# One kernel of linear attention and two gated layers: first loads split, gate work moved between VectorE and GpSimd, and the planner's numbers set anew

## The chip, the cores and the metric

The kernel runs on one core of a Trainium2 chip. The metric is the device time of one execution in microseconds (us). A core has five engines that run their own queues in order: TensorE (PE in the profile, its weight loads PEld), VectorE (DVE), ScalarE (ACT), GpSimd (POOL) and SyncE (SP), which here issues every DMA. They wait for each other through semaphores.

## The reference

Three stages follow each other. All data is float32, except the weights, which arrive as float64.

```python
# attention: B=4, H=8, S=768 steps, D=48
for t in range(S):
    state = alpha[:, :, t, :, None] * state + einsum('bhd,bhe->bhde', k[:, :, t], v[:, :, t])
    y[:, :, t] = einsum('bhd,bhde->bhe', q[:, :, t], state)
x = y with its heads side by side              # 3072 tokens x 384
# first layer, d_ff = 2048
h = x @ w_in
g = (a[0] + a[1]*h + a[2]*h**2 + a[3]*h**3) / (1 + abs(b[0])*abs(h) + abs(b[1])*h**2 + 1e-6)
x = g @ w_out
# second layer, d_ff = 2048
h = x @ w_in2
out = (h * tanh(softplus(h))) @ w_out2
```

## The kernel before, in words

The 768 steps are cut into six blocks of 128, and each block holds 512 tokens (4 batches of 128). Attention of a block is two units (`attn_unit`, two batches each): twelve units in all. Inside a unit the steps stand in chunks of 64, and within a chunk the decays are handled by doubling: six levels (1, 2, 4, 8, 16, 32), at each of which TensorE makes a triangle of scores (line 444), VectorE scales queries and keys by products of decays (lines 451, 457), and VectorE or, for the levels 16 and 32, ScalarE writes the scores into the matrix AT (lines 477, 472, 466). Ahead of the levels stands the product of queries and keys themselves (line 412), and the first scaling of half of the queries by the decays (line 418). After the levels come transposes of the keys (505, copied by ScalarE at 509), the chunk's state (520), the state's decay on GpSimd (529) and its gain on VectorE (534), the outputs (555 or 591), and copies by ScalarE (612, 616) into `xf`, the input of the first layer. For the first unit ScalarE copies the first chunk's state at line 544. Queries (`QC`), keys (`K`) and decays (`al`) of a unit lie in one tile `qka` of 128 x 3 x 1024; the second unit borrows the tile `zp` for it.

A layer runs over a block in 16 steps. A step is nine matmuls of 512 columns into one PSUM bank (`hidden_mms`, line 632), the gate on the other engines, and nine matmuls into three output banks (`out_mms`, line 681). Nine, because float32 is kept by splitting input and weights into a rounded high part and the rest: three products for each of three slices. In the first layer the gate is the rational function: ScalarE takes |h| into `u` (647), B1*|h|+B0 into `z` (653), GpSimd multiplies z by u (654); or, where `E_M` has a V for the block, ScalarE makes B1*|h| from the bank (649) and VectorE adds and multiplies (650). ScalarE makes A3*h (655), VectorE two steps of the polynomial (656, 658), ScalarE log and exp of the denominator (660, 664), VectorE the last step (665). In the second layer it is one activation (669). In both, the result is split (`split_g`): the high part by a cast `gh` (helper line 215 on ScalarE, 217 on VectorE), the rest by a subtraction `gl` (helper line 208 on VectorE, 210 on GpSimd). `E_GL` says by layer and block which of the two engines subtracts.

The weights come as float64 and are converted on the chip during the first blocks: ScalarE (320, 333, 334) and VectorE (336, or 322 to 326) put the bits together, a cast makes the high part, and the low part is made on TensorE with a copy by ScalarE (344, 345, 348) or by a subtraction on VectorE (208), as `E_LW` says. Low parts go to DRAM and are streamed back for each later block.

All of this is recorded first and put in order afterwards by `Plan.order`, a list scheduler: each operation has a due time, worked out from the numbers at the head of the file (`T0`, `T_PH`, `AT_P0`, `LAG` and so on), and on each engine the ready operation with the earliest due time is taken. So the numbers set the order of every queue. The planner also puts small matmuls without use on TensorE's queue (line 725) until the first layer begins. The blocks of the two layers are run in the order of `PHASES`, (layer, block): (0,0), (0,1), (1,0), (0,2), (1,1) and so on, with the attention of the next block between the matmuls.

Of the kernel before, what the change touches and what calls it, by code (L numbers as in the profile page):

```python
# [15 lines left out]
ALU = mybir.AluOpType  # L16
# [9 lines left out]
NTOK = B * P  # L26
# [9 lines left out]
NLVM = 5  # L36
T0 = 34.498
PHASES = ((0, 0), (0, 1), (1, 0), (0, 2), (1, 1), (0, 3), (1, 2), (0, 4), (1, 3), (0, 5), (1, 4), (1, 5))
T_PH = (8.299, 4.563, 4.71, 6.475, 6.278, 6.257, 9.331, 8.784, 5.935, 5.739, 5.256, 2.662)
AT_P0 = (0.424, -13.295, 0.991)  # L40
AT_P1 = (0.528, 1.587, 0.282)
AT_P = (0.554, 1.217, 0.317)
D_MID = 8.38
LAG = (27.598, 7.732)
D_SPL = (1.238, -1.451)
W_LEAD = 13.438
X_LEAD = 139.18
D_W1 = (-0.027, 22.996)
D_W2 = (22.28, 21.655)
E_LO = 'VV'  # L50
E_TREE, E_QK = ('PPPVPV', 'VVVVVP')
E_M = 'PPVPPV'
E_GL = ('PVPVVV', 'VVVVPP')
R_PSUM = [0, 0, 0, 0, 0, 0]
NWL, NWO = 8, 8
N16 = 20
C_PED = 2
N_PRE = 8
E_LW = 'PPPPPPPPVVVVVVVVVVVVVVVVVVVVVVVV'
E_HC = 'AAAAAAAVAAVAAAAAAAAAAVVAAVVVVVVA'  # L60
E_X0 = 'A'
E_CV = 'AAAAAAAAAAAADDDDDDDDDDDDDDAADDAA'
R0 = (34.089, 17.077)
NDIAG = 20
NRAW, NF32 = 2, 2
D_X = 88.596
D_EV = 0.91
F_OPEN = 5.16
F_END = 110.537
F_RATE = 1281.623  # L70
D_CST = -48.973
NZ, NG, NU = 4, 3, 3
# [5 lines left out]
class Plan:  # L78
# [11 lines left out]
    def __init__(self):  # L90
        self.ops, self.writer, self.readers = [], {}, {}
        self.filler = None

# [17 lines left out]
    def order(self):  # L111
        ops = self.ops
# [5 lines left out]
        free, port = {}, 0.0  # L118
        ready = {}
        ops = self.ops = list(ops)  # L120
        events = [(1.9, 1, n) for n in range(len(ops)) if not left[n]]
        heapq.heapify(events)
        out, busy, loaded = [], {}, 0
        fill, lit = self.filler, 1e9
        while events:
            t = events[0][0]
            while events and events[0][0] <= t + 1e-9:
                _, kind, n = heapq.heappop(events)
                if kind == 0 and fill and n == fill[5]:
                    lit = max(fill[1], t + 2.7)  # L130
                    heapq.heappush(events, (lit, 2, -1))
                if kind == 1:
                    heapq.heappush(ready.setdefault(ops[n][0], []), (ops[n][2], n))
            if fill and lit <= t < fill[2] and free.get("PE", 0.0) <= t + 1e-9 and not ready.get("PE"):
                tick = int(t / self.TICK)
                if busy.get(tick, 0) < fill[3] * (t - tick * self.TICK + fill[0]):
                    ops.append(("PE", fill[0], 0.0, set(), fill[4], False, 1.0, None))
                    users.append([])
                    ready.setdefault("PE", []).append((0.0, len(ops) - 1))
                else:  # L140
                    heapq.heappush(events, (t + 0.1, 2, -1))
            for eng, q in ready.items():
# [3 lines left out]
                while q:  # L146
# [7 lines left out]
                    if eng == "PE":  # L154
                        if us == 0.680:
                            fill = None
# [26 lines left out]
def attention_moe_kernel(ctx: ExitStack, tc: tile.TileContext,  # L183
# [35 lines left out]
    def dma(kb, due, reads, writes, emit):  # L219
        plan.add("SP", max(0.42, kb / 300.0), due, reads, writes, emit, False, 2.5)  # L220
# [148 lines left out]
    def attn_unit(b, c, bf, due):  # L369
# [20 lines left out]
        def now():  # L390
            return due(k[0] / steps)

        dma(1573, now() - 8, [], [kQC, kK, kal], lambda: nc.sync.dma_start(out=bf.qka, in_=qka[u]))
        if c >= C_PED:
# [243 lines left out]
    def hidden(l, hb, r, i, due):  # L638
# [7 lines left out]
        if l == 0:  # L646
# [5 lines left out]
            else:  # L652
# [7 lines left out]
            act(NTOK, due, [], [kz], lambda: nc.scalar.activation(zs[r], zs[r], AF.Ln, bias=c_1), src="s", ptr=1, table="ln")  # L660
            kw = kh if R_PSUM[c] else kz
            w = lambda: h if R_PSUM[c] else zs[r]
            act(NTOK, due, [kz], [kw] + (["tab"] if last else []),
                lambda: nc.scalar.activation(w(), zs[r], AF.Exp, scale=-1.0), src="s", table="ln")  # L664
            dve(NTOK, due, [kw], [kp], lambda: nc.vector.scalar_tensor_tensor(  # L665
                out=ps[r], in0=ps[r], scalar=A0, in1=w(), op0=ALU.add, op1=ALU.mult), port=not R_PSUM[c], ptr=1)
        else:
# [195 lines left out]
```

## Time and profile before

| | us |
|---|---|
| median of 3 runs (1012.78 to 1016.35) | 1014.22 |
| the profiled execution | 1018.92 |
| its span, first to last instruction | 1017.1 |
| first matmul of the first layer begins | 80.14 |
| TensorE busy | 977.7 |
| VectorE busy | 653.1 |
| ScalarE busy | 647.4 |
| GpSimd busy | 254.4 |

The profiled execution is one run, 4.7 us above the median of the others. A busy TensorE is not one at full speed: the profile's busy time of a matmul overlaps that of the next, and holds what the clock costs. Idle time of another engine costs nothing as long as TensorE has work.

### The profile page before, as it was taken

The page shows a single profiled execution, that of the slowest core. Times are in us where ns is not written, and L with a number is a line of the kernel's source. Part 1 is how long each engine was busy: PE and PEld are TensorE (multiplying, and loading weights), DVE is VectorE, ACT ScalarE, POOL GpSimd, SP SyncE. Part 2 cuts the span into 40 slices and gives each one's busy share as a digit, 9 for nine tenths or more (in the row PEclk, how much of TensorE's full clock was granted, in tenths as well). Part 3 has the DMA queues.
Part 4 walks back from the last instruction along what each step waited for, and adds up shares of the span by engine and source line. Part 5 has one row for each costly group of instructions (what it writes and reads, how often), then busy time and mean ns, then how long its engine had stood idle before and what let it go on. Part 6 is the DMA issues. An engine that isn't in the chain of part 4 may idle for free.

```text
span 1017.1 us, 25314 instructions
## 1 busy us (share of the span) xinstructions
PE 977.7 (96%) x10744; PEld 788.2 (77%) x10744; DVE 653.1 (64%) x850; ACT 647.4 (64%) x1130; POOL 254.4 (25%) x202
## 2 busy tenths in 40 slices
PE   7999969899999999999999999999999999999998
PEld 6767757678788778888778887878778878888886
DVE  4767799899997799644598633588972379500100
ACT  3899958799887889523489823376712289623432
POOL 2023745533400133101235200143300000033332
PEclk9999989899999999999999999999999999999999
DMA  7565638756688858467638555737554555475530
GB/s 288 164 205 227 203 122 315 246 164 228 211 313 275 306 160 266 138 195 239 196 89 265 173 192 172 227 102 255 150 182 132 162 149 148 139 222 151 166 114 31
DMA packets 74608, 195.28 MB, mean 192 GB/s; under 512 B 8064, under 2 KB 34816, under 8 KB 72960
## 3 DMA queue, kind: packets, MB, share of 16 engines
q1 hardware_dynamic: 74496, 193.68, 59.1%
q8 instruction: 84, 1.38, 0.5%
q14 instruction: 28, 0.23, 0.1%
HBM read 162.19 MB, written 31.46 MB: 190 GB/s over the span
## 4 chain that ended last, share of the span: by engine, by line
PE 57%; DVE 8%; ACT 3%; DMA 3%; issue 2%; SPq 0%; ACTq 0%; DVEq 0%
PE bank L681 27%; PE bank L632 26%; PE pair L444 3%; DMA raw<-in_w2i_dram 2%; PE pair L591 1%; DVE zp L665 1%; DVE gg L208 1%; DMA qka<-in_qka_dram 1%; DVE qka L457 1%; DVE zp L656 1%; DVE AT L477 1%; DVE zp L658 1%; PE pair L505 0%; PE pair L520 0%; ACT u L647 0%
## 5 line engine op out<-in xcount | busy, mean ns | idle before, releaser
L681 PE MATMUL bank<-gg,wo 128*128 128x512 f32 x1728 | 427.6, 392 | 2.8 <-DVE gg L208 1.7
L681 PEld LDWEIGHTS bank<-gg,wo 128*128 128x128 f32 x1728 | 321.0, 188 | 73.5 <-DVE gg L208 4.8
L632 PE MATMUL bank<-xh,wih 128*128 128x512 f32 x576 | 232.7, 404 | 3.9 <-DVE zp L658 2.5
L632 PE MATMUL bank<-xl,wih 128*128 128x512 f32 x576 | 227.5, 395 | 0.9 <-DVE xl L626 0.9
L632 PE MATMUL bank<-xh,wl 128*128 128x512 f32 x576 | 227.1, 394 | 0.0
L669 ACT ACTIVATE zp<-bank 128x512 f32<-128x512 f32 x96 | 57.4, 598 | 208.5 <-PE bank L632 204.9
L210 POOL TENSOR_TENSOR gg<-zp,gg 128x512 fp32r<-128x512 f32 x64 | 89.1, 1394 | 314.0 <-ACT gg L215 284.7
L654 POOL TENSOR_TENSOR zp<-zp,u 128x512 f32<-128x512 f32 x64 | 99.8, 1562 | 171.1 <-ACT zp L653 170.9
L632 PEld LDWEIGHTS bank<-xh,wih 128*128 128x128 f32 x576 | 109.5, 190 | 28.3 <-DVE zp L658 3.4
L632 PEld LDWEIGHTS bank<-xh,wl 128*128 128x128 f32 x576 | 109.7, 190 | 23.4
L632 PEld LDWEIGHTS bank<-xl,wih 128*128 128x128 f32 x576 | 109.6, 190 | 23.4 <-DVE xl L626 2.0
L208 DVE TENSOR_TENSOR gg<-zp,gg 128x512 fp32r<-128x512 f32 x128 | 91.9, 721 | 32.5 <-ACT gg L215 31.1
L215 ACT CAST gg<-zp 128x512 fp32r<-128x512 f32 x144 | 88.7, 620 | 23.3 <-DVE zp L665 10.7
L665 DVE SCALAR_TENSOR_TENSOR zp<-zp,sc 128x512 f32<-128x512 f32 x96 | 84.7, 888 | 10.8 <-ACT zp L664 9.5
L444 PEld LDWEIGHTS pair<-qka 48*64 48x64 f32 (+4 forms) x4224 | 60.8, 128 | 37.8 <-issue 15.6
L656 DVE SCALAR_TENSOR_TENSOR zp<-zp,sc,bank 128x512 f32<-128x512 f32 x96 | 70.5, 740 | 20.1 <-ACT zp L655 19.8
L529 POOL TENSOR_TENSOR tmp<-X,qk 48x768 f32<-48x768 f32 x19 | 30.6, 1613 | 208.9 <-DVE X L534 147.5
L444 PE MATMUL pair<-qka 48*64 48x32 f32 (+4 forms) x4224 | 68.3, 214 | 14.3 <-DVE AT L477 7.1
L660 ACT ACTIVATE zp<-zp,c 128x512 f32<-128x512 f32 x96 | 69.3, 724 | 6.9 <-POOL zp L654 5.6
L658 DVE SCALAR_TENSOR_TENSOR zp<-zp,sc,bank 128x512 f32<-128x512 f32 x96 | 71.1, 743 | 2.4 <-ACT u L647 0.7
L647 ACT ACTIVATE u<-bank 128x512 f32<-128x512 f32 x96 | 57.0, 595 | 23.0 <-PE bank L632 21.0
L655 ACT ACTIVATE zp<-bank,sc 128x512 f32<-128x512 f32 x96 | 66.1, 688 | 7.8 <-PE bank L632 3.0
(118 smaller groups left out, 989.8 us busy)
## 6 DMA issues: line engine op xcount, KB each, us to landing
wo<-woD SPq DMA_DIRECT2D x160, 384.0 KB, 3.3
wl<-wlD SPq DMA_DIRECT2D x160, 192.0 KB, 2.4
qka<-in_qka_dram SPq DMA_DIRECT2D x11, 1536.0 KB, 7.9
woD<-wo SPq DMA_DIRECT2D x16, 768.0 KB, 5.7
raw<-in_w1o_dram SPq DMA_DIRECT2D x8, 768.0 KB, 5.2
raw<-in_w1i_dram SPq DMA_DIRECT2D x8, 768.0 KB, 4.3
wlD<-wl SPq DMA_DIRECT2D x16, 384.0 KB, 5.9
raw<-in_w2i_dram SPq DMA_DIRECT2D x8, 768.0 KB, 6.3
```

The source lines that it names most:

```text
L208: dve(n, due, reads, writes, lambda: nc.vector.tensor_tensor(**kw()))
L210: pool(n, due, reads, writes, lambda: nc.gpsimd.tensor_tensor(**kw()))
L215: act(n, due, reads, writes, lambda: nc.scalar.copy(out=out(), in_=in_()), src="s")
L444: nc.tensor.matmul(bk[j][o:o + m, 32 * g:32 * g + 32].rearrange("p (n l) -> p n l", l=L), lhsT=K[h, e * HC:e * HC + m], rhs=Qv[h, e, :, 1, :],
L632: nc.tensor.matmul(bank[hb], lhsT=w[:, k * P:(k + 1) * P], rhs=x[k], start=(k == 0 and j == 0), stop=(k == KT - 1 and j == 2))
L654: pool(NTOK, due, [ku], [kz], lambda: nc.gpsimd.tensor_tensor(out=zs[r], in0=zs[r], in1=u, op=ALU.mult))
L655: act(NTOK, due, [kh], [kp], lambda: nc.scalar.activation(ps[r], h, AF.Copy, scale=A3), ptr=1)
L656: dve(NTOK, due, [kh], [kp], lambda: nc.vector.scalar_tensor_tensor(out=ps[r], in0=ps[r], scalar=A2, in1=h, op0=ALU.add, op1=ALU.mult), po ...
L658: dve(NTOK, due, [kh], [kp], lambda: nc.vector.scalar_tensor_tensor(out=ps[r], in0=ps[r], scalar=A1, in1=h, op0=ALU.add, op1=ALU.mult), po ...
L660: act(NTOK, due, [], [kz], lambda: nc.scalar.activation(zs[r], zs[r], AF.Ln, bias=c_1), src="s", ptr=1, table="ln")
L665: dve(NTOK, due, [kw], [kp], lambda: nc.vector.scalar_tensor_tensor(out=ps[r], in0=ps[r], scalar=A0, in1=w(), op0=ALU.add, op1=ALU.mult), ...
L681: nc.tensor.matmul(bank[5 + k], lhsT=wos[b][:, w, k * P:(k + 1) * P], rhs=x[q], start=(f == 0 and j == 0), stop=(f == FT - 1 and j == 2))
```

## The change

Three things are edited by hand. For the two units of the first block the tile `qka` is loaded by two DMAs, queries and keys first, decays second, instead of by one. The string for the first layer's subtractions becomes V for all six blocks (before: GpSimd for the first and third), and the second layer's becomes `VVPPVP` (before `VVVVPP`). The product z*u of the third block goes to GpSimd. Besides, single conversions change engine: the low part of the first tile of the first output weights is made by VectorE (before: TensorE and ScalarE), the three casts of the first block's input are made by VectorE (before: ScalarE), two later weight casts go from ScalarE to VectorE, and two conversions swap their form. `R_PSUM` and the planner's filler are written differently with the same meaning. All due times of the planner have new numbers, and these move operations on every queue.

```diff
-T0 = 34.498
+T0 = 38.697
-T_PH = (8.299, 4.563, 4.71, 6.475, 6.278, 6.257, 9.331, 8.784, 5.935, 5.739, 5.256, 2.662)
+T_PH = (7.975, 4.763, 4.733, 6.876, 6.684, 6.257, 9.56, 8.784, 5.759, 6.787, 4.726, 2.36)
...
-E_M = 'PPVPPV'
-E_GL = ('PVPVVV', 'VVVVPP')
-R_PSUM = [0, 0, 0, 0, 0, 0]
+E_M = 'PPPPPV'
+E_GL0 = 'VVVVVV'
+E_GL1 = 'VVPPVP'
+R_PSUM = '......'
...
-E_LW = 'PPPPPPPPVVVVVVVVVVVVVVVVVVVVVVVV'
-E_HC = 'AAAAAAAVAAVAAAAAAAAAAVVAAVVVVVVA'
-E_X0 = 'A'
-E_CV = 'AAAAAAAAAAAADDDDDDDDDDDDDDAADDAA'
+E_LW = 'PVPPPPPPVVVVVVVVVVVVVVVVVVVVVVVV'
+E_HC = 'AAAAAAAVAAVAAAAAAAAAVVVAVVVVVVVA'
+E_X0 = 'V'
+E_CV = 'AAAAAAAAAAAADDDDDDDDDDDDDAADDDAA'
...
-        dma(1573, now() - 8, [], [kQC, kK, kal], lambda: nc.sync.dma_start(out=bf.qka, in_=qka[u]))
+        if c == 0:
+            dma(1049, now() - 8, [], [kQC, kK], lambda: nc.sync.dma_start(out=bf.qka[:, 0:2], in_=qka[u, :, 0:2]))
+            dma(524, now() - 8, [], [kal], lambda: nc.sync.dma_start(out=al, in_=qka[u, :, 2]))
+        else:
+            dma(1573, now() - 8, [], [kQC, kK, kal], lambda: nc.sync.dma_start(out=bf.qka, in_=qka[u]))
...
-        tt(E_GL[l][c], NTOK, due, [kp, kgh], [kgl],
+        tt((E_GL0, E_GL1)[l][c], NTOK, due, [kp, kgh], [kgl],
            lambda: dict(out=gls[q], in0=ps[r], in1=ghs[q].bitcast(F32), op=ALU.subtract))
```

In the pieces of the queues below a line number is the old one plus 1 ahead of the split load and plus 5 behind it: 208 becomes 209, 457 becomes 462, 544 becomes 549.

First, ScalarE's queue at the copy of the second unit's state (`X_141`, line 544). `wo_93` and `wih_3` are weight tiles in conversion, `zp` the second unit's keys, `xf` the first unit's outputs. Before:

```order
L348 CAST wo_93<-bank_131 128x384
L334 ACTIVATE zb_103<-raw_99,c_f 128x768
L509 COPY zp<-bank_127 128x512
L509 COPY zp<-bank_128 128x512
L348 CAST wo_93<-bank_132 128x384
L320 ACTIVATE f_102<-raw_100 128x768
L215 CAST wih_3_74<-f_101 128x768
L333 ACTIVATE zb_104<-raw_100 128x768
L544 COPY X_141<-bank_127 48x8x48
L334 ACTIVATE zb_104<-raw_100,c_f 128x768
L544 COPY X_141<-bank_128 48x8x48
```

and now:

```order
L514 COPY zp<-bank_127 128x512
L335 ACTIVATE zb_103<-raw_99,c_f 128x768
L621 COPY xf<-pair 128x3x128 x2
L514 COPY zp<-bank_128 128x512
L349 CAST wl_89<-bank_130 128x384
L349 CAST wo_93<-bank_131 128x384
L321 ACTIVATE f_101<-raw_99 128x768
L334 ACTIVATE zb_104<-raw_100 128x768
L549 COPY X_141<-bank_127 48x8x48
L349 CAST wo_93<-bank_132 128x384
L549 COPY X_141<-bank_128 48x8x48
L216 CAST wih_3_74<-f_101 128x768
```

The second unit's state now stands ahead of the cast of `wih_3` and the second half of `wo_93`, and the first unit's outputs stand later, beside it.

Second, VectorE's queue from the last scaling of the second unit (line 457, `zp`) to the gain of its state (`X_142`); `qka_145` and `AT_144` belong to the third unit, the first of the next block. Before:

```order
L457 TENSOR_TENSOR zp<-zp,xg 128x2x16x32
L418 TENSOR_TENSOR qka_145<-qka_145 128x512
L424 COPY_PREDICATED AT_144<-cst,pair 128x1024
L336 SCALAR_TENSOR_TENSOR f_101<-f_101,zb_103 128x768
L451 TENSOR_TENSOR qka_145<-qka_145 128x1024
L477 COPY_PREDICATED AT_144<-cst,pair 128x512
L336 SCALAR_TENSOR_TENSOR f_102<-f_102,zb_104 128x768
L477 COPY_PREDICATED AT_144<-cst,pair 128x256x2
L534 TENSOR_TENSOR X_142<-tmp,bank_127 48x8x48
```

and now:

```order
L462 TENSOR_TENSOR zp<-zp,xg 128x2x16x32
L337 SCALAR_TENSOR_TENSOR f_101<-f_101,zb_103 128x768
L429 COPY_PREDICATED AT_144<-cst,pair 128x1024
L423 TENSOR_TENSOR qka_145<-qka_145 128x512
L539 TENSOR_TENSOR X_142<-tmp,bank_127 48x8x48
```

Three rows of the third unit's levels (four operations) and one conversion no longer stand ahead of the second unit's state: of seven rows between, three remain.

Third, VectorE's queue in the first layer's first block, at the last scalings of the fourth unit: levels 16 and 32 are the two rows 32x16 and 16x32; 322 to 326 are conversions, 665 and 658 steps of the gate. Before:

```order
L457 TENSOR_TENSOR qka_145<-qka_145,qk_148 128x2x64x8
L665 SCALAR_TENSOR_TENSOR zp<-zp,sc 128x512
L322 TENSOR_SCALAR f_101<-f_101 128x768
L322 TENSOR_SCALAR f_102<-f_102 128x768
L457 TENSOR_TENSOR qka_145<-qka_145,qk_148 128x2x32x16
L324 SCALAR_TENSOR_TENSOR f_101<-raw_99,f_101 128x768
L324 SCALAR_TENSOR_TENSOR f_102<-raw_100,f_102 128x768
L326 SCALAR_TENSOR_TENSOR f_101<-raw_99,f_101 128x768
L326 SCALAR_TENSOR_TENSOR f_102<-raw_100,f_102 128x768
L457 TENSOR_TENSOR qka_145<-qka_145,qk_148 128x2x16x32
```

and now:

```order
L462 TENSOR_TENSOR qka_145<-qka_145,qk_148 128x2x64x8
L482 COPY_PREDICATED AT_144<-cst,pair 128x64x8
L661 SCALAR_TENSOR_TENSOR zp<-zp,sc,bank_129 128x512
L670 SCALAR_TENSOR_TENSOR zp<-zp,sc 128x512
L323 TENSOR_SCALAR f_101<-f_101 128x768
L462 TENSOR_TENSOR qka_145<-qka_145,qk_148 128x2x32x16
L209 TENSOR_TENSOR gg<-zp,gg 128x512
L325 SCALAR_TENSOR_TENSOR f_101<-raw_99,f_101 128x768
L663 SCALAR_TENSOR_TENSOR zp<-zp,sc,bank_129 128x512
L327 SCALAR_TENSOR_TENSOR f_101<-raw_99,f_101 128x768
L670 SCALAR_TENSOR_TENSOR zp<-zp,sc 128x512
L462 TENSOR_TENSOR qka_145<-qka_145,qk_148 128x2x16x32
```

Between the scalings of levels 16 and 32 four conversions become two, and two steps of the gate and a subtraction (209 to `gg`, formerly GpSimd's) come in: four rows become five.

## Rows read from the trace of the kernel before

**Rows 1.** Page: busy us (share) xcount by engine; granted clock in tenths, 40 slices:

```profile
PE 977.7 (96%) x10744; PEld 788.2 (77%) x10744; DVE 653.1 (64%) x850; ACT 647.4 (64%) x1130; POOL 254.4 (25%) x202
...
PEclk9999989899999999999999999999999999999999
```

**Rows 2.** 20-us stretches (length): PE, PEld, DVE, ACT, POOL busy, clock, DMA share, GB/s:

```profile
20.00:40.00 20.00, 19.67 (x534) 14.77 (x533) 17.55 (x21) 15.05 (x23) 0.67 (x3) 0.94 0.32 99
...
60.00:80.00 20.00, 17.14 (x517) 13.22 (x515) 14.35 (x16) 17.87 (x28) 6.62 (x8) 1.00 0.68 225
80.00:100.00 20.00, 19.86 (x203) 15.97 (x204) 15.06 (x20) 18.68 (x36) 8.38 (x7) 0.91 0.57 211
100.00:120.00 20.00, 19.89 (x268) 16.30 (x267) 14.84 (x19) 20.00 (x36) 14.36 (x11) 1.00 0.55 188
120.00:140.00 20.00, 19.54 (x320) 15.26 (x318) 19.93 (x23) 15.04 (x23) 14.62 (x12) 1.00 0.44 134
140.00:160.00 20.00, 11.71 (x225) 9.73 (x226) 17.38 (x19) 11.93 (x21) 5.92 (x4) 0.74 0.60 203
```

**Rows 3.** Chain of work that ended last, near its end: start, length, what:

```profile
1005.34 2.04 PE bank L632 x9
```

**Rows 4.** Timeline of PE: start, length, operation, [idle before and its releaser]:

```profile
9.04 1.16 PE L412 MATMUL pair<-qka 48*64 48x64 f32 x64
...
80.14 0.50 PE L632 MATMUL bank<-xh,wih 128*128 128x512 f32 x1 [1.36 <-ACT xh L215]
```

**Rows 5.** Timeline of SP's queue, an issue:

```profile
1.65 0.42 SPq L393 DMA_DIRECT2D qka<-in_qka_dram  x1
```

**Rows 6.** Timeline of VectorE, first unit:

```profile
10.27 0.69 DVE L418 TENSOR_TENSOR qka<-qka 128x512 f32<-128x512 f32 x1 [7.25 <-PE pair L412]
```

**Rows 7.** Groups of ScalarE, 43.3 to 78 us: busy us, mean ns, idle before:

```profile
L334 ACT ACTIVATE zb<-raw,c_f 128x768 uint16<-128x768 uint16 x7 | 8.2, 1167 | 0.1
...
L333 ACT ACTIVATE zb<-raw 128x768 f16<-128x768 f32 x6 | 6.5, 1085 | 2.0 <-DMA raw<-in_w1i_dram 1.8 <-DMA raw<-in_w1o_dram 0.3
...
L348 ACT CAST wo<-bank 128x384 fp32r<-128x384 f32 x5 | 2.4, 487 | 0.0
...
L472 ACT COPY zp<-bank 16x128 f32<-16x128 f32 x8 | 2.0, 253 | 0.1
```

**Rows 8.** Timeline of ScalarE:

```profile
21.41 0.48 ACT L348 CAST wo<-bank 128x384 fp32r<-128x384 f32 x1 [3.64 <-PE bank L345]
...
42.42 0.79 ACT L544 COPY X<-pair 48x768 f32<-48x768 f32 x1 [0.18 <-PE pair L520]
...
66.12 0.47 ACT L544 COPY X<-bank 48x384 f32<-48x384 f32 x1
...
77.15 0.82 ACT L616 COPY xf<-bank 128x384 f32<-128x384 f32 x2
...
78.89 1.64 ACT L215 CAST xh<-xf 128x512 fp32r<-128x512 f32 x3
```

**Rows 9.** Page's costliest groups: subtractions of the gates:

```profile
L210 POOL TENSOR_TENSOR gg<-zp,gg 128x512 fp32r<-128x512 f32 x64 | 89.1, 1394 | 314.0 <-ACT gg L215 284.7
...
L208 DVE TENSOR_TENSOR gg<-zp,gg 128x512 fp32r<-128x512 f32 x128 | 91.9, 721 | 32.5 <-ACT gg L215 31.1
```

**Rows 10.** Timeline of PE, first block:

```profile
144.28 0.75 PE L444 MATMUL pair<-qka 48*32 48x32 f32 x64 [2.97 <-DVE qka L457]
...
149.96 1.94 PE L505 MATMUL pair<-cst,qka 128*128 128x128 f32 x8 [4.93 <-DVE qka L457]
```

**Rows 11.** Timeline of VectorE, first block:

```profile
134.46 2.03 DVE L208 TENSOR_TENSOR wo<-f,wo 128x768 fp32r<-128x768 f32 x1
...
148.60 1.21 DVE L457 TENSOR_TENSOR qka<-qka,qk 128x1024 f32<-128x1024 f32 x1
...
150.60 0.94 DVE L208 TENSOR_TENSOR wo<-f,wo 128x768 fp32r<-128x768 f32 x1
```

**Rows 12.** Timeline of GpSimd, first block:

```profile
135.63 2.02 POOL L654 TENSOR_TENSOR zp<-zp,u 128x512 f32<-128x512 f32 x1
```

More of the change, by code (lines that the diff above doesn't have):

```diff
@@ L36 @@
 NLVM = 5
-T0 = 34.498
+T0 = 38.697
 PHASES = ((0, 0), (0, 1), (1, 0), (0, 2), (1, 1), (0, 3), (1, 2), (0, 4), (1, 3), (0, 5), (1, 4), (1, 5))
-T_PH = (8.299, 4.563, 4.71, 6.475, 6.278, 6.257, 9.331, 8.784, 5.935, 5.739, 5.256, 2.662)
[L40 to L49, printed above, removed]
+T_PH = (7.975, 4.763, 4.733, 6.876, 6.684, 6.257, 9.56, 8.784, 5.759, 6.787, 4.726, 2.36)
+AT_P0 = (0.516, -13.056, 0.934)
+AT_P1 = (0.531, 1.929, 0.294)
+AT_P = (0.554, 1.16, 0.317)
+D_MID = 8.19
+LAG = (31.563, 9.121)
+D_SPL = (0.045, -1.21)
+W_LEAD = 12.177
+X_LEAD = 122.716
+D_W1 = (0.938, 24.112)
+D_W2 = (21.44, 21.127)
 E_LO = 'VV'
 E_TREE, E_QK = ('PPPVPV', 'VVVVVP')
-E_M = 'PPVPPV'
-E_GL = ('PVPVVV', 'VVVVPP')
-R_PSUM = [0, 0, 0, 0, 0, 0]
+E_M = 'PPPPPV'
+E_GL0 = 'VVVVVV'
+E_GL1 = 'VVPPVP'
+R_PSUM = '......'
 NWL, NWO = 8, 8
@@ L58 @@
 N_PRE = 8
-E_LW = 'PPPPPPPPVVVVVVVVVVVVVVVVVVVVVVVV'
-E_HC = 'AAAAAAAVAAVAAAAAAAAAAVVAAVVVVVVA'
-E_X0 = 'A'
-E_CV = 'AAAAAAAAAAAADDDDDDDDDDDDDDAADDAA'
-R0 = (34.089, 17.077)
+E_LW = 'PVPPPPPPVVVVVVVVVVVVVVVVVVVVVVVV'
+E_HC = 'AAAAAAAVAAVAAAAAAAAAVVVAVVVVVVVA'
+E_X0 = 'V'
+E_CV = 'AAAAAAAAAAAADDDDDDDDDDDDDAADDDAA'
+R0 = (35.647, 12.613)
 NDIAG = 20
 NRAW, NF32 = 2, 2
[L66 to L69, printed above, removed]
+D_X = 82.539
+D_EV = -8.761
+F_OPEN = 6.894
+F_END = 101.015
 F_RATE = 1281.623
-D_CST = -48.973
+D_CST = -51.722
 NZ, NG, NU = 4, 3, 3
@@ L91, in __init__ @@
         self.ops, self.writer, self.readers = [], {}, {}
-        self.filler = None
+        self.fill = None
     def add(self, eng, us, due, reads, writes, emit, port=False, after=0.0, table=None):
@@ L123, in order @@
         out, busy, loaded = [], {}, 0
-        fill, lit = self.filler, 1e9
+        fill, filler = self.fill, None
         while events:
@@ L128, in order @@
                 _, kind, n = heapq.heappop(events)
-                if kind == 0 and fill and n == fill[5]:
-                    lit = max(fill[1], t + 2.7)
-                    heapq.heappush(events, (lit, 2, -1))
+                if kind == 0 and n == fill[4]:
+                    filler = fill[5]
+                    heapq.heappush(events, (max(fill[1], t + 2.7), 2, -1))
                 if kind == 1:
                     heapq.heappush(ready.setdefault(ops[n][0], []), (ops[n][2], n))
-            if fill and lit <= t < fill[2] and free.get("PE", 0.0) <= t + 1e-9 and not ready.get("PE"):
+            if filler and fill[1] <= t < fill[2] and free.get("PE", 0.0) <= t + 1e-9 and not ready.get("PE"):
                 tick = int(t / self.TICK)
                 if busy.get(tick, 0) < fill[3] * (t - tick * self.TICK + fill[0]):
-                    ops.append(("PE", fill[0], 0.0, set(), fill[4], False, 1.0, None))
+                    ops.append(("PE", fill[0], 0.0, set(), filler, False, 1.0, None))
                     users.append([])
@@ L155, in order @@
                         if us == 0.680:
-                            fill = None
+                            filler = None
                         tick = int(t / self.TICK)
@@ L660, in hidden @@
             act(NTOK, due, [], [kz], lambda: nc.scalar.activation(zs[r], zs[r], AF.Ln, bias=c_1), src="s", ptr=1, table="ln")
-            kw = kh if R_PSUM[c] else kz
-            w = lambda: h if R_PSUM[c] else zs[r]
+            kw = kh if R_PSUM[c] == "R" else kz
+            w = lambda: h if R_PSUM[c] == "R" else zs[r]
             act(NTOK, due, [kz], [kw] + (["tab"] if last else []),
@@ L665, in hidden @@
             dve(NTOK, due, [kw], [kp], lambda: nc.vector.scalar_tensor_tensor(
-                out=ps[r], in0=ps[r], scalar=A0, in1=w(), op0=ALU.add, op1=ALU.mult), port=not R_PSUM[c], ptr=1)
+                out=ps[r], in0=ps[r], scalar=A0, in1=w(), op0=ALU.add, op1=ALU.mult), port=R_PSUM[c] != "R", ptr=1)
         else:
@@ L725, in warm @@
         nc.tensor.matmul(bank[4][:, 0:2 * P], lhsT=ident, rhs=cst[:, 0:2 * P], start=True, stop=True)
-    plan.filler = (0.44, F_OPEN, F_END, F_RATE, warm, plan.writer["cst"])
+    plan.fill = (0.44, F_OPEN, F_END, F_RATE, plan.writer["cst"], warm)
     def attend(c):
```

## The prediction

> **What bounds the kernel now.** I read the busy times by engine first, then the stretches of 20 us, then the chain of waits, then timelines where TensorE falls short. TensorE is busy for 977.7 us of 1017.1 [rows 1]; at the end of the chain nine large matmuls take 2.04 us [rows 3], and there are 384 such groups (12 passes of 16 steps, two groups each), so 783 us is the floor of the two layers alone. The shortfall sits at the front. The first layer's first matmul starts at 80.14 us, released by ScalarE's cast of the input [rows 4]. Up to there TensorE's queue holds the attention of the first block and matmuls without use, so what matters is the chain through the two units, and behind the first 20 us this chain runs in ScalarE's queue: it is busy for 17.87 of 20 us from 60 on [rows 2]. From 80 to 140 TensorE is busy for 19.5 to 19.9 of 20 us; from 140 to 160 only for 11.71, with a granted clock of 0.74 [rows 2]. There it waits for VectorE's scalings (line 457), 2.97 us and 4.93 us [rows 10]. VectorE is busy for 19.93 us of the 20 before that [rows 2]. So a change can gain at the front, through ScalarE's queue and the first loads, and in the first layer's first blocks, through VectorE; and this one adds work to VectorE just there.
>
> **The start.** The load of the first unit is issued at 1.65 us [rows 5], its first matmul starts at 9.04 [rows 4]. By bytes (176 KB of constants ahead, 1024 of 1536 KB needed) queries and keys would be there at 1.65 + 7.39 * 1200/1712 = 6.8 us, an estimate. But VectorE's first scaling, at 10.27 behind the scores [rows 6], needs the decays too, and these come one issue (0.42 us) later than now, at about 9.4. It gains 0.8 us; the bounds are 0 and 10.27 - 9.04 = 1.2 us.
>
> ScalarE's queue is the larger part. Between the copy of the first unit's state (ends 43.2 us) and the second unit's last copy to the layer's input (ends 77.97) [rows 8] it has 56 instructions now and 43 in the changed order: two fewer of line 334 (1.167 us), two of 333 (1.085), five of 348 (0.487) and four of 472 (0.253) [rows 7]. That is 2.3 + 2.2 + 2.4 + 1.0 = 7.9 us, or 7.0 as neighbours overlap a little (two copies of line 616 take 0.82 us together, and three casts 1.64 [rows 8]). The first queue piece shows it at the second unit's state, which is copied at 66.12 us now [rows 8]. The instructions aren't gone: two each of 333, 334 and 348 and four of 472, 6.5 us, stand ahead of the first unit's state instead. ScalarE has room there: 4.95 us idle from 20 to 40 [rows 2] and most of a wait of 3.64 us, which ended at 21.41 and was for a low part on TensorE that VectorE now makes [rows 2, 8]. I let the first state come 1.5 us later than now, with the 0.8 us of the load already taken off; bounds 0 and 6.5. Last, the casts of the input leave ScalarE, where the first stands behind a conversion and starts at 78.89 [rows 8]. VectorE's cast is not in the rows; between nothing and ScalarE's 0.55 us each, with a price near the latter, the first matmul gains 0.7 us. Sum: -7.0 + 1.5 - 0.7 = -6.2 us, so the first layer begins at about 74. Bounds: 0 (all of it lost to the earlier conversions) and -9.5.
>
> **What TensorE still owes.** Before the first layer's first matmul the queue had 17 level passes and has 15. A pass takes 0.75 us [rows 10] to 1.2 (the 1.16 of line 412 [rows 4]). From 80 to 120 TensorE has no idle time to hide two passes [rows 2], so +2.0 us, bounds 1.5 and 2.4. By the eighth step both orders have done the same work on TensorE.
>
> **The subtractions of the first block.** Sixteen go from GpSimd (1.394 us) to VectorE (0.721) [rows 9]: 11.5 us more on VectorE. By the order one conversion (three operations of up to 0.94 us) slips behind the block, so about +9. In the 80 us from 80 to 160 VectorE idles for 4.94 + 5.16 + 0.07 + 2.62 = 12.8 us [rows 2], most of it before 120. I take 1.5 us as exposed, nearer to the cover than to the full price, because seven of the sixteen fall into the first eight steps, where the idle time is. Bounds: +9 (no cover), and -3 where GpSimd no longer holds VectorE up.
>
> **The wait at 144 to 150.** In the third queue piece the work between the scalings 16 and 32 costs as much as now (four conversions of about 0.94 us against two, a subtraction and two gate steps of 0.7), so VectorE is no earlier. But in its order TensorE now has three groups of three output matmuls among its last two level passes and the transposes, where it had none: 3 * 0.68 = 2.0 us of work in place of waiting. -2.0 us; bounds 0, and -10 if the 7.9 us go and the clock stays up (0.26 of 20 us was lost to the granted clock in this stretch, half of it in time).
>
> **Edits at nothing.** In the third block the first layer's products and subtractions change places between GpSimd and VectorE, 16 each way, at nearly equal prices. In the second layer 32 subtractions go to GpSimd and 16 come back; the matmuls there have a step's 4.08 us for each subtraction of 1.39 [rows 3, 9], and at the end of the kernel, where all are on GpSimd, the chain is matmuls without a gap. If that cover is gone, a subtraction costs 0.67 us each, 11 us a block at the most. The rest of the order changes in many places by a step or less; I give it 0, plus or minus 3.
>
> **Sum.** -6.2 + 2.0 + 1.5 - 2.0 = -4.7 us. The profiled execution took 1018.92 us, so 1014.2 for it; the median of the runs is 4.7 us lower, 1014.22, and there the forecast is 1009.5 us.
>
> **Rivals.** *Given back.* The start gains 4 us net, but the units of the second block don't move with it: VectorE at 19.93 of 20 us from 120 to 140 [rows 2] says that its queue is the bound there, 12.8 us of idle time ahead of it speaks against. The added work is then exposed by 4 or 5 us, and the time is 1014, as before.
>
> *VectorE becomes the bound.* It begins with the subtractions behind 120 us: if none of the added 9 us finds the idle time of 80 to 120, the sum is -6.2 + 2.0 + 9 = +4.8 us, and the subtraction between scaling 16 and 32 makes the wait there longer by 0.7: 1014.2 + 5.5 = 1019.7 us. It decides as soon as more than the start's 4.2 us are exposed. For it speaks that VectorE runs its queue in order, so an addition ahead of a scaling delays the unit; against it, that a subtraction on VectorE is ready 0.67 us sooner for TensorE.
>
> *GpSimd lets go.* A low part of 768 elements took VectorE 2.03 us at 134.46 while GpSimd was in its products, and 0.94 at 150.60, when it was not [rows 11, 12]. The Trainium skill (SBUF — State Buffer, section Who interferes with whom) says that a VectorE instruction with two SBUF inputs and a GpSimd instruction that reads SBUF exclude each other for the whole instruction; these two rows agree with that. With sixteen instructions of 1.39 us gone from the first block [rows 9], VectorE gets back up to 22 us of such exclusion. If a third of them met one, 7 us come back, and the added 9 cost 2 while the scalings come on time: with the wait at 144 to 150 and its low clock gone (-8 instead of -2), the sum is -6.2 + 2.0 + 2 - 8 = -10.2 us, 1004 us. Against it: the rows show one such pair, and ScalarE's and TensorE's parts of the waits stay.
>
> That the split load does nothing, because the matmuls wait for both parts, would cost 0.8 us of the sum, and is inside the forecast's own range.
>
> **Chances.** Forecast 0.48, given back 0.17, VectorE the bound 0.17, GpSimd lets go 0.18. Runs of this kernel tell about 0.3% from no change, 3 us: faster is below 1011.2, slower above 1017.3. Of the forecast's own range, 1006 to 1013, three quarters are faster; with nearly all of the last rival that makes 0.36 + 0.02 + 0.18 = 0.56 faster, 0.12 + 0.13 + 0.02 = 0.27 the same, and 0.17 slower. The range that holds 8 in 10 runs from the last rival to the third, with a little less on both sides of the unknown prices: 1002 to 1020.
>
> **What would show it.** In the profile of the changed kernel: the first line-417 matmul at about 7 us and the first scaling near 9.5; the copies of `X_141` at about 60 us, the first large matmul at 72 to 76 (80 would refute the start); VectorE near 20 of 20 us from 100 on, and the waits of TensorE for scalings shorter between the tenth and thirteenth step. The distance from the first large matmul to the end of the span was 937.0 us (1017.1 - 80.1); the forecast wants 938 to 939. If it is 943 or more, VectorE's load took the gain; below 934, GpSimd's release was worth more than I think.

## The result and the profile after

The changed kernel took 1019.28 us (median of 8 runs, 1017.72 to 1023.61); the kernel before, beside it, 1014.84 (8 runs). The ratio is 1.0051, 95% interval 1.0032 to 1.0070: slower, where the forecast was 1009.5. In a later set of runs the ratio was 1.0022 (0.9994 to 1.0050), while a second build of the kernel before, the control, came to 1.0030 (1.0004 to 1.0057) against its equal. So the loss lies between nothing and 0.7%, a gain of 0.5% is refuted, and of the ratios below two that differ by 0.3% or less are not told apart by the times. One kernel's runs follow the mean granted clock: the control took 1010.0 us at 0.995 and 1021.93 at 0.983.

The profiled execution took 1018.90 us with a span of 1017.1, as before's 1018.92 and 1017.1. That pair hides the loss, for before's profiled run was longer than all eight of its timed ones. I therefore put two profiles of each kernel side by side, by the starts of the large matmuls:

| stretch, us | before | second build | after | second build |
|---|---|---|---|---|
| to the first large matmul | 80.1 | 82.3 | 81.0 | 79.8 |
| first layer, blocks 0 and 1 | 171.6 | 171.9 | 170.0 | 172.4 |
| the next two phases (second layer, block 0; first layer, block 2) | 161.4 | 159.8 | 162.7 | 162.5 |
| the next three (second layer, block 1; first, 3; second, 2) | 240.6 | 239.9 | 238.3 | 238.3 |
| first layer, block 4 (from about 652) | 79.1 | 77.2 | 79.6 | 80.8 |
| the rest | 284.4 | 284.4 | 285.4 | 285.4 |

The start gains about 0.8 us where 6.2 was forecast, and from 252 us on the changed kernel loses 3.1 (766.0 and 766.9 against 765.4 and 761.3) where I had put nothing. Profiles of the experiments below bear this out: behind 252 us three more of the changed order take 765.7 to 767.1, a third of before's order 759.3. That makes 4.3 us on average, though before's three differ by 6.

The page of the kernel after, busy times and clock [rows 1], and its stretches of 20 us (columns as in [rows 2]):

```profile
PE 981.8 (97%) x10746; PEld 790.4 (78%) x10746; DVE 649.1 (64%) x856; ACT 646.3 (64%) x1125; POOL 271.3 (27%) x202
```

```profile
20.00:40.00 20.00, 18.19 (x548) 14.45 (x547) 17.55 (x22) 12.89 (x18) 2.77 (x4) 0.91 0.36 118
80.00:100.00 20.00, 18.80 (x266) 14.70 (x264) 19.26 (x26) 17.35 (x31) 5.21 (x3) 1.00 0.62 252
120.00:140.00 20.00, 18.18 (x313) 13.91 (x311) 18.63 (x21) 15.81 (x26) 12.40 (x11) 1.00 0.42 139
140.00:160.00 20.00, 17.38 (x303) 12.93 (x303) 19.62 (x24) 11.67 (x21) 1.70 (x2) 0.83 0.58 192
```

TensorE is busy for 17.38 us from 140 to 160 where it was 11.71 [rows 2] (17.05 and 11.20 in the second builds): the waits that I looked at did shrink. Where before waited 2.97 and 4.93 us for scalings [rows 10], no wait for a scaling (line 462) is left from 130 to 170 us; TensorE now waits for VectorE's subtractions, for less:

```profile
138.75 1.42 PE L686 MATMUL bank<-gg,wo 128*128 128x512 f32 x5 [0.29 <-DVE gg L209]
...
148.37 1.22 PE L686 MATMUL bank<-gg,wo 128*128 128x512 f32 x2 [1.05 <-DVE gg L209]
```

But ScalarE, which I wanted to fill up early, is busy for 12.89 us from 20 to 40 where it was 15.05.

TensorE at the start of the kernel after [rows 4]:

```profile
7.27 1.99 PE L417 MATMUL pair<-qka 48*64 48x64 f32 x64 [1.39 <-DMA qka<-in_qka_dram]
9.19 3.63 PE L730 MATMUL bank<-cst 128*128 128x256 f32 x10
12.74 1.13 PE L449 MATMUL pair<-qka 48*64 48x32 f32 x64
```

The scores come 1.8 us earlier than 9.04, but their 64 matmuls take 1.99 us where they took 1.16 [rows 4]. Then ten matmuls without use take 3.63 us, and the first level pass stands at 12.74 (12.49 in before). The split load's gain is gone after 5 us: over the profiles named further down, five of the changed order and four of before's, that pass comes at 12.75 and at 12.77 on average.

ScalarE of the kernel after [rows 8]: three early waits, then the copies of the first and the second unit's state:

```profile
17.28 0.83 ACT L216 CAST wo<-f 128x768 fp32r<-128x768 f32 x1 [4.01 <-DVE f L337]
23.37 0.92 ACT L321 ACTIVATE f<-raw 128x768 f32<-128x768 f32 x1 [1.58 <-DMA raw<-in_w1o_dram]
28.46 0.83 ACT L216 CAST wih<-f 128x768 fp32r<-128x768 f32 x1 [4.18 <-DVE f L337]
48.57 0.79 ACT L549 COPY X<-pair 48x768 f32<-48x768 f32 x1
65.53 0.47 ACT L549 COPY X<-bank 48x384 f32<-48x384 f32 x1
```

The two casts in the kernel before:

```profile
16.94 0.83 ACT L215 CAST wo<-f 128x768 fp32r<-128x768 f32 x1 [3.70 <-DVE f L336]
28.96 0.83 ACT L215 CAST wih<-f 128x768 fp32r<-128x768 f32 x1 [2.38 <-DVE f L336]
```

The first state comes 6.15 us after 42.42. The idle time that was to swallow the earlier conversions is still there. The longest wait for TensorE fell from 3.64 us [rows 8] to 0.95, but the two waits for VectorE's part of the conversions stayed (8.2 us together; 6.1 in before, 8.0 in the second builds of both), and waits of 0.75 and 1.58 us for loads of weights came in.

The two places of the loss behind 252 us, TensorE of the kernel after:

```profile
283.55 0.73 PE L686 MATMUL bank<-gg,wo 128*128 128x512 f32 x2 [1.58 <-ACT u L699]
```
```profile
696.75 1.11 PE L596 MATMUL pair<-qka,X 48*48 48x64 f32 x64 [3.15 <-DVE X L539]
```

The same place in the second build of before, and in that of the changed kernel:

```profile
693.61 1.11 PE L591 MATMUL pair<-qka,X 48*48 48x64 f32 x64 [0.24 <-DVE X L534]
```
```profile
697.67 1.96 PE L596 MATMUL pair<-qka,X 48*48 48x64 f32 x64 [3.17 <-DVE X L539]
```

Line 539 (534) is the gain of the last half unit's state. What VectorE does ahead of it in the kernel after, and GpSimd beside it:

```profile
691.55 2.07 DVE L218 CAST gg<-zp 128x512 fp32r<-128x512 f32 x1
693.54 0.73 DVE L663 SCALAR_TENSOR_TENSOR zp<-zp,sc,bank 128x512 f32<-128x512 f32 x1
694.20 0.73 DVE L661 SCALAR_TENSOR_TENSOR zp<-zp,sc,bank 128x512 f32<-128x512 f32 x1
694.97 0.75 DVE L663 SCALAR_TENSOR_TENSOR zp<-zp,sc,bank 128x512 f32<-128x512 f32 x1
695.75 0.95 DVE L539 TENSOR_TENSOR X<-tmp,pair 48x768 f32<-48x768 f32 x1
```
```profile
691.04 2.29 POOL L211 TENSOR_TENSOR qk<-qk 128x768 f32<-128x768 f32 x1 [0.57 <-DMA qk<-in_nat_dram]
```

Three steps of the gate stand ahead of the gain, and a cast that takes 0.41 us two casts earlier takes 2.07 beside GpSimd's product. Behind the wait TensorE runs at the lower of its levels (1.2 GHz, a granted clock of 0.5), in both profiles of the changed kernel (the second from 696.6). Of before's two profiles the first has such a half-clock stretch too, 3.4 us from 681.3, the second none:

```profile
697.70:701.10 3.40, 3.27 (x79) 2.78 (x69) 2.83 (x5) 1.07 (x2) 0.00 (x0) 0.51 0.64 184
```
```profile
696.60:703.40 6.80, 5.59 (x132) 4.95 (x133) 4.86 (x9) 1.07 (x2) 0.00 (x0) 0.50 0.41 136
```

### The profile page after: what moved, and what is told of

It reads as the page before. It is cut to its first block, busy times and chain, and to the rows that moved or that the text cites. A ratio compares the mean times of both kernels' runs of the same rounds, so it can differ in the third digit from the quotient of the medians.

```text
span 1017.1 us, 25296 instructions
## 1 busy us (share of the span) xinstructions
PE 981.8 (97%) x10746; PEld 790.4 (78%) x10746; DVE 649.1 (64%) x856; ACT 646.3 (64%) x1125; POOL 271.3 (27%) x202
## 4 chain that ended last, share of the span: by engine, by line
PE 69%; DVE 16%; ACT 8%; issue 3%; DMA 3%; POOL 1%; SPq 0%; ACTq 0%; DVEq 0%
PE bank L686 30%; PE bank L637 29%; PE pair L449 3%; DVE zp L670 2%; DVE qka L462 2%; DVE zp L661 2%; DVE gg L209 2%; DVE zp L663 2%; PE pair L596 2%; DVE AT L482 1%; PE bank L730 1%; ACT zp L658 1%; POOL zp L659 1%; ACT zp L665 1%; ACT u L652 1%
## 5 line engine op out<-in xcount | busy, mean ns | idle before, releaser
L686 PEld LDWEIGHTS bank<-gg,wo 128*128 128x128 f32 x1728 | 321.5, 189 | 77.9 <-DVE gg L209 7.3
L659 POOL TENSOR_TENSOR zp<-zp,u 128x512 f32<-128x512 f32 x80 | 135.4, 1695 | 250.8 <-ACT zp L658 250.4
L209 DVE TENSOR_TENSOR gg<-zp,gg 128x512 fp32r<-128x512 f32 x144 | 104.4, 729 | 61.1 <-ACT gg L216 60.0
L211 POOL TENSOR_TENSOR gg<-zp,gg 128x512 fp32r<-128x512 f32 x48 | 64.9, 1353 | 278.4 <-ACT gg L216 222.5
L670 DVE SCALAR_TENSOR_TENSOR zp<-zp,sc 128x512 f32<-128x512 f32 x96 | 82.0, 860 | 10.0 <-ACT zp L669 9.2
```

What stands on the lines that cost most here:

```text
L659: pool(NTOK, due, [ku], [kz], lambda: nc.gpsimd.tensor_tensor(out=zs[r], in0=zs[r], in1=u, op=ALU.mult))
L686: nc.tensor.matmul(bank[5 + k], lhsT=wos[b][:, w, k * P:(k + 1) * P], rhs=x[q], start=(f == 0 and j == 0), stop=(f == FT - 1 and j == 2))
```

## The experiments

Ratios are to the kernel before on the same chip. Moves are made in the finished order, so that nothing else changes place.

**The control, and the changed kernel again.** No edit.

> The kernel before once more, for a second profile and for what two equal programs differ by. All theories: 1014 us, ratio 1.000 within 0.002, first large matmul at 80 us (79.5 to 80.8), 937 us from there to the end. If the first large matmul or the distance to the end moves by more than 1.5 us, the pair of profiles is too coarse to tell a few us apart, and stages have to be read from several profiles.

> The changed kernel once more. All theories: ratio 1.005 to the kernel before, first large matmul at 81 us. The theory of the start (the conversions that now stand ahead of the first unit's state on ScalarE cost what the shorter queue behind it gains) wants 0.5 to 1.5 us of the loss ahead of the first large matmul and the rest behind it. The theory of the clock (matmuls without use at half clock at the start, and other half-clock stretches later) wants half-clock stretches at the same places as in the first profile (25 to 29, 53 to 59, 148 to 155 us).

Measured: 1.0030 (1.0004 to 1.0057) and 1.0022 (0.9994 to 1.0050). The first large matmul moved by 2.1 us between the two builds of before and by 1.2 between those of after, so single profiles don't tell 2 us apart at the start. The changed kernel's half-clock stretches at the start moved too (25 to 29 and 53 to 59 us, then 24 to 28 and 79 to 86); the one at 697 stayed.

**The parts.** Only the split load; only the planner's numbers.

> The kernel before with only the load of the first block's units split. Prediction's term: first scaling 0.8 us earlier than 10.27, and as nothing else moves, first large matmul 0 to 0.8 us earlier than 80.1; ratio 0.999 to 1.000 (1013.4 to 1014.2). The rival (the second DMA issue pushes the constants, weights and raw loads behind it on SyncE, so what follows the first scaling is no earlier): first large matmul at 80.1 to 80.6, ratio 1.000 to 1.001.

> The kernel before with all of the planner's new numbers, and none of the three edits by hand nor the changed engines. If the new order alone is what loses (the conversions ahead of the first state, the order of later blocks): ratio 1.003 to 1.010, first unit's state copied at 46 to 49 us, first large matmul at 80 to 83 us. If VectorE's added subtractions lose it: ratio 0.995 to 1.000 with these numbers, and the distance from the first large matmul to the end at or below 937 us.

```diff
 split load alone:  + the two-DMA branch, before's numbers
 numbers alone:     + T0 ... D_CST of after, before's engines and load
```

Measured: 1.0034 (1.0011 to 1.0057) for the load, as the control: nothing. The first scaling came at 9.1 us, but two more instructions in the plan dealt the order anew (first state at 44.9, second at 62.2, first large matmul at 78.5), so this is not the load alone. For the numbers 1.0061 (1.0035 to 1.0086): the new order is slower than before without any of the engines moved, though its interval overlaps the control's. Its profile, the slowest of its ten runs, loses elsewhere than the changed kernel does: the first large matmul comes at 87.9 us behind a 17 us stretch at a granted clock of 0.50, there is no wait of 3 us at the last half unit's gain, and from the second layer's first matmul on it takes 763.1 us. So the numbers alone do not make the late waits; the moved engines without the numbers were not run.

**Three operations moved.** 2685 is the state's gain, 2684 the matmuls it needs, 2861 a gate step, 1084 the copy of the third output bank near 282 us.

```diff
+        for n, m in ((2685, 2684), (2861, 2685), (1084, 1080)):
+            out.remove(n)
+            out.insert(out.index(m) + 1, n)      # n right behind m
```

> The changed kernel with three operations moved in its order and nothing else: VectorE's gain of the last half unit's state (near 695 us) goes ahead of the three gate steps that stand before it, and the copy of the third output bank after the first layer's second block (near 282 us) goes ahead of the conversion before it on ScalarE. Theory of the late waits (the loss against before stands in two waits of TensorE that the new order makes, 3.15 us at 697 and 1.4 to 1.6 us at 283, the first with a stretch at half clock behind it): both waits shrink by 2.1 and 1.5 us, no half-clock stretch near 697, TensorE's idle time from 652 to 732 us falls from 5.3 to about 3, the distance from the second layer's first matmul at 252 us to the end from 766.0 and 766.9 us to 760.5 to 763; the time is 3.6 us below the changed kernel's, up to 6 with the clock: 1013 to 1015.5. Rival (the waits are cover for something else and come back in the next step): the distance stays at 765 or more, time 1018 to 1020.

Measured: 1016.87 us, 1.0010 (0.9990 to 1.0030), by the times not told from the changed kernel's 1.0022. The profile tells them apart: from the second layer's first matmul to the end it takes 762.6 us where the five profiles without these moves take 765.7 to 767.1. The stretch from 652 takes 76.8 us (79.6 and 80.8), the wait at 283 is gone, and no half-clock stretch follows the other:

```profile
692.69 1.11 PE L599 MATMUL pair<-qka,X 48*48 48x64 f32 x64 [1.06 <-DVE X L542]
```
```profile
692.70:700.00 7.30, 7.16 (x150) 6.09 (x151) 7.23 (x11) 2.95 (x5) 1.37 (x1) 1.00 0.75 236
```

The theory of the late waits holds, for somewhat less than the time it wanted (1013 to 1015.5).

**The start.** Eight conversions, with what depends on them, go behind the copies of the second unit's level 32; then both sets of moves together.

```diff
+        end = out.index(95)
+        late = {139, 149, 150, 138, 153, 154, 155, 164}
+        for n in out[:end]:
+            if ops[n][3] & late: late.add(n)
+        head = [n for n in out[:end + 1] if n not in late]
+        out = head + [n for n in out[:end + 1] if n in late] + out[end + 1:]
```

> The changed kernel with eight conversions of weights, and what depends on them, put behind the second unit's last copies of level 32 in the order (43 to 55 us), ahead of which stand the copies of the first unit's state. Theory of the start (conversions ahead of the first unit's state on ScalarE ate the gain): the first unit's state is copied at 45.5 to 47 us where it was 48.4 to 48.6, its outputs start 2 to 3 us earlier, and the first large matmul comes at 77 to 79 us where it was 79.8 and 81.0; the time is 1 to 3 us lower. Rival (ScalarE's work as a whole up to the input's last copy is the bound, so that an order of it among the two units changes nothing): the state comes earlier, but the second unit's state and the first large matmul stay at 62.6 to 65.5 and 80 to 81 us. The clock's rival (how long TensorE runs at half clock at the start decides): the first large matmul follows the half-clock stretches, 3.4 us each, and not the state.

> Both sets of moves together. If both theories hold the sum is 5 to 8 us below the changed kernel, 1011 to 1014, at or below the kernel before (1014 to 1016). If only the late waits hold: as that kernel, 1013 to 1015.5. If neither: 1018 to 1020.

Measured: 1.0073 (1.0044 to 1.0101) and 0.9994 (0.9973 to 1.0016). First state at 47.3 and 44.2, second at 68.4 and 65.0, first large matmul at 85.2 and 80.7. Earlier for the first unit is later for the second: 21 us between the states in both, where the changed order has 14.2 to 17.0. The rival holds: order among the two units gains nothing.

**ScalarE's work taken away.** Lines 334 and 335 of two weight tiles are not issued.

```diff
-            act(n, due, [kr], [kz], lambda: nc.scalar.activation(...
+            act(n, due, [kr], [kz], lambda: None if nth in (4, 5) else nc.scalar.activation(...
```

> The changed kernel in its order, but four of ScalarE's conversions (lines 334 and 335 of two weight tiles, 1.08 and 1.17 us each, between 36 and 47 us, ahead of the first unit's state) are left out, so these two weight tiles hold wrong numbers. 4.5 us less work for ScalarE. Theory of the start now (ScalarE's work ahead of the input's last copy, wherever it stands among the two units, sets the first large matmul; the idle time that it has early takes none of it): the first state comes at 43 to 45 us (48.4 to 46.6 in the changed order), and the first large matmul at 75 to 77.5 us (78.8 to 81.0). Rival (the chain through TensorE, VectorE and GpSimd sets the start, and ScalarE's queue only looked busy): the first state 0 to 1 us earlier and the first large matmul at 78.5 to 81. Time: 2.5 to 4.5 us lower than the changed kernel, or no different.

Measured: 1016.23 us, 1.0009 (0.9991 to 1.0027), by the times not told from the changed kernel. First state at 45.9, first large matmul at 76.9, against means of 47.7 and 79.5 in five profiles of the changed order (this kernel, its second build, the two with late moves, and the next). Of 4.5 us 1.8 reach the first state and 2.6 the first large matmul. But this profile has no half-clock stretch before 144 us, and against the one of the five that has none before 77.6 us (the last experiment's, 47.0 and 77.9) only 1.1 and 1.0 us are left. So a quarter to somewhat over half of the work shows, and neither theory holds alone. Ahead of the first state ScalarE's waits grew instead; there it waits for TensorE:

```profile
43.11 0.25 ACT L477 COPY zp<-bank 16x128 f32<-16x128 f32 x1 [1.13 <-PE bank L449]
```

**The subtractions alone, with the order kept.** In the changed kernel the first block's sixteen go back to GpSimd; in the kernel before they go to VectorE, and then those of the third block too.

```diff
+        if (l, c) == (0, 0):        # before: (0, 0), then also (0, 2), on nc.vector
+            dve(NTOK, due, [kp, kgh], [kgl], lambda: nc.gpsimd.tensor_tensor(...))
```

> The changed kernel in exactly its order, but the sixteen subtractions of the first layer's first block are made by GpSimd again instead of VectorE. Prediction's term (VectorE's added subtractions cost 1.5 us exposed): 1.5 us lower than the changed kernel, 1017 to 1018, and a later first matmul of the second block if the subtraction on GpSimd, 0.67 us longer, is waited for. Theory that GpSimd's release is worth more: 3 to 10 us slower than the changed kernel, with longer waits of TensorE for VectorE's scalings between 120 and 160 us (idle time of the first block's stretch back from 5.8 to 6.1 us to 9 or 10, as in the kernel before). VectorE's busy time from 80 to 175 us falls by 11 us in any case.

> The kernel before in exactly its order, with the sixteen subtractions of the first layer's first block made by VectorE instead of GpSimd. Prediction's term: 1.5 us slower than before (bounds 9 slower to 3 faster), 1016 to 1017. Theory of the release, as the changed kernel with GpSimd's subtractions was 3 us slower: 2 to 4 us faster than before, 1011 to 1013.5, the waits of TensorE for line 457 between 140 and 156 us shorter than 2.97 and 4.75 us.

> As that, and the sixteen subtractions of the first layer's third block on VectorE too. The prediction gave the third block's exchange nothing. If GpSimd's release is worth as much in each block: 4 to 7 us faster than before, 1008.5 to 1011.5. If VectorE has cover only in the first block: as with the first block alone, or 1 to 3 us slower than that, with longer waits of TensorE for VectorE between 340 and 410 us.

Measured: 1.0068 (1.0041 to 1.0094), 1.0011 (0.9994 to 1.0029) and 1.0039 (1.0017 to 1.0061). In the changed order the kernel with GpSimd's subtractions takes 1022.44 us, 3.8 above the changed kernel's second build, with intervals that overlap a little. The profile shows the cost: from the first large matmul to the second layer's first it takes 174.1 us (169.6 to 172.5 in the seven others with the changed order or moves in it), and TensorE waits for GpSimd directly, where it waited 0.29 and 1.05 us for VectorE:

```profile
139.27 2.41 PE L690 MATMUL bank<-gg,wo 128*128 128x512 f32 x5 [1.95 <-POOL gg L681]
...
149.47 1.10 PE L690 MATMUL bank<-gg,wo 128*128 128x512 f32 x2 [1.83 <-POOL gg L681]
```

In before's order the exchange gains nothing. The second build of before, and then the one with the first block's subtractions on VectorE:

```profile
147.04 0.93 PE L444 MATMUL pair<-qka 48*32 48x32 f32 x64 [2.97 <-DVE qka L457]
152.72 1.94 PE L505 MATMUL pair<-cst,qka 128*128 128x128 f32 x8 [4.75 <-DVE qka L457]
165.32 1.15 PE L555 MATMUL pair<-X,qka 48*64 48x48 f32 x64 [0.74 <-DVE X L534]
```
```profile
144.48 0.83 PE L444 MATMUL pair<-qka 48*32 48x32 f32 x64 [1.91 <-DVE qka L457]
149.09 1.94 PE L505 MATMUL pair<-cst,qka 128*128 128x128 f32 x8 [3.78 <-DVE qka L457]
159.97 0.50 PE L632 MATMUL bank<-xh,wl 128*128 128x512 f32 x1 [0.79 <-DVE wl L208]
163.76 1.96 PE L555 MATMUL pair<-X,qka 48*64 48x48 f32 x64 [2.60 <-DVE X L534]
```

The waits for scalings fall by 2.0 us, and VectorE's work that slipped behind gives 2.7 back. From the first large matmul to the second layer's first both profiles with the exchange take 174.5 us, those without it 171.6 and 171.9, so in this order it costs some 2.8 us there, which the whole time does not show. With the third block's subtractions moved too the ratio is higher by 2.8 us (1.0039 against 1.0011, intervals overlapping), and that block's stretch takes 72.3 us for 70.2 (71.6 and 70.3 in before's two). The third block's product z*u stayed on VectorE in this run, where the change gives it to GpSimd, so this is only half of the exchange that I had put at nothing.

**Four more moves of the late kind.** 2750 is a gate step, 2696 GpSimd's product beside the slow cast (2713 depends on it), 1171 a conversion.

```diff
+        ... (2750, 2804), (1171, 1076), (2696, 2896), (2713, 2696)):
```

> The changed kernel with the late moves, and three more of the same kind: a last step of the gate (near 667 us) goes behind the two steps that free the bank for the next large matmuls; GpSimd's first products of decays for the last unit (near 689 us, beside which a cast on VectorE took 2.07 us and not 0.41) go behind its next product of the gate, into GpSimd's idle time; a conversion near 267 us goes behind two subtractions. If the waits are as free as the first two were: TensorE's waits of 1.67, 1.06 and 0.71 us go, the stretch from 652 to 732 us takes 74 to 75.5 us (76.8 with the first moves, 79.6 and 80.8 without), and the time is 1013 to 1015. If VectorE's work as a whole is the bound there, the waits come back a step later: 76.5 to 77 us and 1015 to 1017.

Measured: 1014.17 us, 0.9976 (0.9958 to 0.9993): some 4.7 us below the changed kernel's 1.0022, the intervals just apart. Against before it is 0.24%, less than the control's 0.30%, so a gain over the kernel before is not shown. The stretch from 652 takes 75.5 us. TensorE, and VectorE's cast and gain without GpSimd beside them:

```profile
690.79 1.11 PE L599 MATMUL pair<-qka,X 48*48 48x64 f32 x64
```
```profile
688.82 0.41 DVE L221 CAST gg<-zp 128x512 fp32r<-128x512 f32 x1
689.27 0.95 DVE L542 TENSOR_TENSOR X<-tmp,pair 48x768 f32<-48x768 f32 x1
```

## Why the prediction was wrong

**The start, forecast -6.2.** The failed step is "I let the first state come 1.5 us later than now". It came 5.0 later (mean 47.7 in the five profiles; 42.7 in four of before's order, with those of the subtractions). I had read ScalarE's idle time as room. By its timeline from 5 us up to the first state it is busy for 21.0 us and idle for 16.4 in before, busy for 26.2 and idle for 17.4 in after; over the four and the five profiles the idle time is the same to 0.1 us. So the work was added and no idle time taken up. The rows suggest why: the waits stand inside the conversions' own chain, for VectorE's part and for the loads, and come again with the next tile. That is not shown to be all, as taking 4.5 us of the work away brought the state only 1.1 to 1.8 us forward. The bound I had named, 6.5, was nearer to the truth than my 1.5.

The other half of the step was right: from the first state's copy to the end of the second unit's last copy to the input 29.0 us on average where it was 35.5, so -6.5 against my -7.0. The casts of the input, -0.7, gained nothing. The first cast itself ends 0.46 us behind that copy where it was 1.52, but the first large matmul comes 2.4 us behind the cast's end where it was 0.9. So my reading "released by ScalarE's cast of the input" failed: neither kernel's first large matmul waits for the cast alone (last section). The load's -0.8 was there at the first scaling (9.32 for 10.27), and nothing behind it came sooner. Together -1.2: 79.5 us where I had said 74.

**What is owed, the subtractions, the wait at 144 to 150** (+2.0, +1.5, -2.0). From the first large matmul to the second layer's first the changed order takes as long as before to half a microsecond (170.0 and 172.4; 171.6 and 171.9), some 2 us less than my sum. TensorE's idle time in the first block, added up from its timeline, falls from 9.4 and 10.2 us to 5.8 and 6.1, so the wait gave more than the -2.0. The subtractions gain some 3 us of this stretch in the changed order and cost some 2.8 in before's, each by one or two profiles; my +1.5 was wrong in sign here, and my rival of GpSimd's release right in direction. But what is seen is TensorE's wait for GpSimd's slow queue, not VectorE freed.

**Edits at nothing, 0 plus or minus 3.** Measured +3.1 from the two pairs, +4.3 over more profiles: the other half of the miss. I had cost the new order behind 200 us by its number of operations and their cover, without asking which single wait of TensorE it would make. It made two, and three moved operations took most of it back. Of the third block's exchange, which I gave nothing, only the half that burdens VectorE was run, and what it costs is not clear of the noise.

The Trainium skill (SBUF — State Buffer, section Who interferes with whom) says that a cast in VectorE's two-port form and GpSimd exclude each other for the whole instruction. The cast of 2.07 us beside GpSimd's 2.29, and of 0.41 with that product moved, agree; the trace does not show in which form the cast ran.

My rival "VectorE becomes the bound" named 1019.7 us, next to the 1019.28 measured. That is luck: it kept the start's gain, which did not come, and wanted 9 us of added subtractions exposed, while in this order they gained time.

Of my signs, the first scaling near 9.5 and the shorter waits between the tenth and thirteenth step came, and the first large matmul "at 72 to 76 (80 would refute the start)" refuted it. The distance from there to the end (936.1 and 939.3; before 937.0 and 933.1) spreads by as much as I wanted to read from it. Open stays what else holds the first state back: more than half of the work taken off ScalarE did not show there, and the half-clock stretches at the start differ from run to run.

## What to carry to other kernels

Idle time of an engine that waits inside a chain is not room: more work of the same chain brings its waits along, so count a step moved ahead at its full time until a row shows otherwise. Where numbers re-deal a whole order, look for the single operation that the bounding engine will wait for and what stands ahead of it in its queue; moving seven operations here was worth nearly 5 us, and the whole new set of numbers gained nothing. Profile each kernel twice before reading 2 us from a pair.

## What the runs showed of the hardware

Right ahead of the first large matmul TensorE stops in all five profiles of the changed order, inside a level pass and with no releaser, four times for 1.84 to 2.20 us (0.79 in the first). The second build of the changed kernel, and its DMA queues from 76 to 79.4 us (packets, MB, share of 16 engines):

```profile
79.47 0.41 PE L449 MATMUL pair<-qka 48*60 48x32 f32 x3 [2.20 <-issue]
```
```profile
q1 hardware_dynamic: 335, 1.39, 99.8%
q8 instruction: 1, 0.02, 1.7%
```

One packet of instructions falls into the stop, while the DMA engines are full of weights. The page of before counts them:

```profile
q8 instruction: 84, 1.38, 0.5%
```

That is one packet for each 256 of its 21488 matmuls and weight loads, or 128 matmuls, an estimate from the page's counts. Over all 14 profiles TensorE stops 38 times for more than 0.3 us with no releaser (up to 1005 us), and each of these stops ends 1.2 to 1.6 us after such a packet has ended. All but two stand at the 224th, 352nd, 480th, 863rd, 1628th or 1629th matmul, which lie whole multiples of 128 apart to within three. In before's order the first large matmul is the 1757th, the next place in this row. It starts 1.5 us after a packet has ended in all four profiles, while the cast that is named as releaser ended 0.65 us ahead of it in the first and 1.36 in the second. So the wait that I ascribed to the casts is by these counts, in part or whole, the loading of TensorE's code, in both kernels. No run was made to test that.
